# MLP steps ahead of value products, one load issue earlier, and V's second copy by DMA, in a fused block-sparse attention and MLP kernel

## The chip, the cores and the metric

The kernel runs on one core of a Trainium2 chip. The metric is the device time of one execution in microseconds (us). The kernel before takes 303.8 us (median of three runs, 303.51 to 305.62). A profile of one execution comes with each kernel. Its span is about 2 us shorter than the device time.

In the text PE is TensorE, ACT ScalarE, DVE VectorE, POOL GpSimd, and SPq the queue of SyncE, from which most DMAs are issued. L433 is line 433 of the kernel.

## The reference

Block-sparse attention for 4 batches x 8 heads x 768 rows x 64 columns, then a low-rank mixer over the sequence and an MLP, with residuals:

```python
scores = scale * q @ k.T                       # masked by block: window, first/last, sampled
attn   = softmax(where(mask, scores, -1e9))
x      = (attn @ v), heads side by side        # 4 x 768 x 512
h      = x.T @ U @ V                           # U 768x32, V 32x768
u      = x + h.T
out    = u + relu(u @ w_ch1) @ w_ch2           # 512 -> 2048 -> 512
```

## The kernel before

Heads go in pairs; a batch has four pairs, and there are 16. A pair has nine units. For each unit PE makes scores (`psc`), ACT their exps (`est`), DVE multiplies the exps by the mask (`est <- est, m`), and PE makes value products (`pav`). DVE normalises these (`rcp`, `xs`), POOL casts them (`xh`), PE makes the mixer's first product (`pa`), DVE casts that (`a`), PE makes the second (`ph`), and DVE adds (`xf`). The MLP of a finished batch (`pt`, relu to `tT`, `pch`, last add `of`) is cut into steps that fill PE during the next batch's attention. In the first batch no exps are multiplied by a mask: extra rows beside q and k (mask rows in `qa`, one-hot rows in `ka`) bring the mask into the score matmuls, and they too come by DMA.

Each engine works through its instructions in the order in which they were recorded, so the order of the Python statements is the schedule. From the second batch on, units go two to a group (the first eight singly), and this loop records a group:

```python
    while gi < len(groups) or work or beside:
        made = []
        for i, u in groups[gi] ...:                # PE: scores; ACT: exps
            scores(i, u, est); made.append((i, u, est))
        while beside and beside[0][0] <= gi:       # PE: ph;  DVE: two xf adds
            beside.popleft()[1]()
        for _ in range(...):                       # DVE: masks of the group before
            i, u, est = unmasked.popleft()
            mask_mul(u, est)
            if u == NU - 1:
                steps = pair_tail(i, *live.pop(i))
                for at, fn in zip((0, 1, 3), steps):   # values c=0, values c=1, pa
                    work.append((gi + at, fn))
                beside.append((gi + 4, steps[3]))      # ph
        unmasked.extend(made)
        ...                                        # loads, casts, transposes
        while work and work[0][0] <= gi:           # PE: pav or pa
            work.popleft()[1]()
        if gi in OPENS:
            fill.extend(mlp_steps(OPENS.index(gi)))
        if fill:                                   # PE: MLP steps
            run_fill(...)
```

The loads of the first pairs, and V, which is wanted at partitions 0 to 31 (`Vt`, `Vd`) and again at 64 to 95 (`Vd`):

```python
    def at_unit(i, u):
        if i == 0:
            if u == 0:
                cast(1, "q"); cast(1, "k"); cast(1, "v")     # POOL  (cut)
            if u == 1:
                ...
                issue(2, "qk")                               # SPq
                for h in range(2):                           # mask and one-hot rows, pair 1
                    keep(nc.sync.dma_start(out=qa[1][h][mrows[h], :], in_=qa[0][h][mrows[h], :]))
                    hot_rows(nc.sync, 1, h, D)
                issue(2, "v")
                for h in range(2):                           # V twice from memory
                    keep(nc.sync.dma_start(out=mvld[h * D : h * D + R], in_=moe_V))
                ...
        if u == 0 and i == 1:
            for o in (Vt[0:R], Vd[0:R]):
                keep(nc.gpsimd.tensor_copy(out=o, in_=mvld[0:R].rearrange("r (p t) -> r t p", t=T)))
        if u == 0 and i == 2:
            keep(nc.gpsimd.tensor_copy(out=Vd[D : D + R], in_=mvld[D : D + R].rearrange(...)))
```

The softmax here doesn't subtract the row's maximum and nothing guards it: scores larger than these inputs give would overflow.

Of the kernel before, what the change touches and what calls it, by code (L numbers as in the profile page):

```python
# [10 lines left out]
FP32 = mybir.dt.float32  # L11
# [10 lines left out]
def kernel(  # L22
# [12 lines left out]
    nc = tc.nc  # L35

    B, H, S, D = q.shape
    BLK = 32
    NB = S // BLK
    T = S // P  # L40
    HD = H * D
    HP = H // 2
    R = moe_U.shape[1]
# [51 lines left out]
    keep = tc.keep_in_program_order  # L95
# [50 lines left out]
    Vt = wpool.tile([P, T, P], FP16)  # L146
    Vd = wpool.tile([P, T, P], FP16)
    w1t = wpool.tile([P, NCC, CH], FP16)
    small = w1t[:, 0, 0 : S + 2 * NB]
    w2t = wpool.tile([P, NJJ, HD], FP16)  # L150
# [18 lines left out]
    def issue(i, names="qkv"):  # L169
        if i >= NPAIR:  # L170
            return
        for nm in names:
            keep(nc.sync.dma_start(out=new_ld(i, nm), in_=src_of(nm, i)))

    def cast(i, nm):
        if i >= NPAIR:
            return
        b, hp = divmod(i, HP)
        ld = lds.pop((i, nm))
        if nm == "v":  # L180
            keep(
                nc.gpsimd.tensor_copy(  # L182
                    out=vts[b % 2][:, 2 * hp : 2 * hp + 2, :, 0:D], in_=ld
                )
            )
            return
        st = stpool.tile([P, T, 2, D], FP16, tag="st" + nm, name=nm + "st")
        keep(nc.gpsimd.tensor_copy(out=st.rearrange("p t h d -> p h t d"), in_=ld))  # L188
        sts[i, nm] = st
# [34 lines left out]
    def hot_rows(eng, st, h, n):  # L224
# [5 lines left out]
            out=sbi[0:NB].rearrange("z r w -> z (r w)"),  # L230
            in_=sampled_blocks.bitcast(I32),
# [20 lines left out]
    def warm_pe(n):  # L252
        for _ in range(n):
            mm(
                warm.rearrange("p (r n) -> p r n", r=4), zeros,
                zeros[:, None, :].broadcast_to([P, 4, P]), True, True,
            )
# [5 lines left out]
            out=eq[0:NB],  # L263
# [7 lines left out]
            out=cb[0:NB],  # L271
            in_=eq[0:NB].rearrange("z r c -> z c r"),
# [6 lines left out]
            out=cbd[0:NB, :, 0:NB],  # L279
# [77 lines left out]
    cast(0, "v")  # L357

    uld = w2t[:, 3, 0 : 2 * T * R].bitcast(FP32)
    mvld = w2t[:, 0:3, :].rearrange("r j d -> r (j d)").bitcast(FP32)  # L360

    def load_w1(cc):
        keep(
# [331 lines left out]
    def at_unit(i, u):  # L695
        if (i, u) in MASKS:
            mask_tiles(MASKS.index((i, u)))
        if i == 0:
            if u == 0:
                warm_pe(2)  # L700
                cast(1, "q")
                cast(1, "k")
                cast(1, "v")
            if u == 1:
                turn_some(qst, pq, TQ, T)
                for h in range(2):
                    half_copy(nc.vector.tensor_copy, qa[0], h, pq, TQ, T)
                turn_some(kst, pk, TK, T)
                for h in range(2):
                    half_copy(nc.vector.tensor_copy, ka[0], h, pk, TK, T)  # L710
                give_back(pq, 0.0)
                give_back(pk, 0.0)
                give_back(warm, 0.0)
                issue(2, "qk")
                for h in range(2):
                    keep(
                        nc.sync.dma_start(
                            out=qa[1][h][mrows[h], :], in_=qa[0][h][mrows[h], :]
                        )
                    )  # L720
                    hot_rows(nc.sync, 1, h, D)
                issue(2, "v")
                for h in range(2):
                    keep(
                        nc.sync.dma_start(out=mvld[h * D : h * D + R], in_=moe_V)
                    )
                keep(
                    nc.sync.dma_start(
                        out=uld, in_=moe_U.rearrange("(p t) r -> p (t r)", t=T)
                    )  # L730
                )
            if u == 3:
                issue(3)
            if u == 6:
                cast(2, "q")
                cast(2, "k")
                cast(2, "v")
            if u == 4:
                turn_part(1, "q", 0)
                turn_part(1, "q", 1)  # L740
            if u in (5, 6):
                turn_part(1, "k", u - 5)
            return
        if u == 0:
            issue(i + 3)
            if i == 1:
                for h in range(2):
                    keep(
                        nc.gpsimd.tensor_copy(
                            out=Ut[:, :, h * D : h * D + R],  # L750
                            in_=uld.rearrange("p (t r) -> p t r", t=T),
                        )
                    )
                for o in (Vt[0:R], Vd[0:R]):
                    keep(
                        nc.gpsimd.tensor_copy(
                            out=o, in_=mvld[0:R].rearrange("r (p t) -> r t p", t=T)
                        )
                    )
            if i == 2:  # L760
                keep(
                    nc.gpsimd.tensor_copy(
                        out=Vd[D : D + R],
                        in_=mvld[D : D + R].rearrange("r (p t) -> r t p", t=T),
                    )
                )
        if (i, u) in WLOADS:
            WLOADS[i, u]()
        if u in (1, 2, 3, 4):
            turn_part(i + 1, "qk"[(u - 1) // 2], (u - 1) % 2)  # L770
        if u == 6:
            cast(i + 2, "q")
            cast(i + 2, "k")
        if u == 8:
            cast(i + 2, "v")
        for _ in range({0: 1, 5: 2, 6: 1, 7: 1}.get(u, 0)):
            if tails:
                tails.popleft()()
# [17 lines left out]
    def run_fill(us):  # L796
        state["debt"] += us
        while fill and state["debt"] > 0:
            cost, fn = fill.popleft()
            fn()  # L800
            state["debt"] -= cost
        if not fill:
            state["debt"] = min(state["debt"], 0.0)
# [34 lines left out]
    work = deque()  # L838
    beside = deque()
    gi = 0  # L840
    while gi < len(groups) or work or beside:
        made = []
        for i, u in groups[gi] if gi < len(groups) else []:
            b, hp = divmod(i, HP)
            if u == 0:
                if hp == 0:
                    start_batch(b)
                live[i] = ([], *new_x())
            est = new_est()
            live[i][0].append(est)  # L850
            scores(i, u, est)
            made.append((i, u, est))
        while beside and beside[0][0] <= gi:
            beside.popleft()[1]()
        for _ in range(len(unmasked) if gi >= SINGLE else 2 if gi >= OPENS[0] else 0):
# [4 lines that stand above are left out]
                for at, fn in zip((0, 1, 3), steps):  # L860
                    work.append((gi + at, fn))
                beside.append((gi + 4, steps[3]))
        unmasked.extend(made)
        for i, u, est in made:
            if u == 0:
                if i > HP:
                    turn_dma(i + 1, "q")
                    turn_dma(i + 1, "k")
                issue(i + 3)
            if u == 3:  # L870
                cast(i + 2, "q")
            if u == 5:
                cast(i + 2, "k")
            if u == 7:
                cast(i + 2, "v")
        if gi == 0:
            flush_value()
            tails.popleft()()
            flush_value()
        if gi == 1:  # L880
            flush_value()
            put_off.pop(0)()
        if gi == 2:
            tails.popleft()()
            tails.popleft()()
            put_off.pop(0)()
        if gi == 3:
            tails.popleft()()
            tails.popleft()()
        if gi == 5:  # L890
            tails.popleft()()
        if gi == 6:
            while put_off:
                put_off.pop(0)()
        while work and work[0][0] <= gi:
            work.popleft()[1]()
        if gi in OPENS:
            fill.extend(mlp_steps(OPENS.index(gi)))
        if fill:
            to_come = [n for n in OPENS if n > gi] or [gi + 1]  # L900
            run_fill(sum(c for c, _ in fill) / (to_come[0] - gi))
        if gi == 6:
            for nm in "qk":
                for part in range(2):
                    turn_part(HP + 1, nm, part)
        gi += 1
# [35 lines left out]
```

## Time and profile before

I divide the span at two points: where the first batch's MLP matmuls run on after their last wait (53.26 us), and where the last batch's begin (256.89 us).

| stage | from, to | length | what leads |
|---|---|---|---|
| first | 0 to 53.26 us | 53.3 us | loads, then exps on ACT |
| middle | to 256.89 us | 203.6 us | PE, with waits |
| last | to 302.2 us | 45.3 us | PE alone, MLP |

The page of the kernel before, part 1 (busy us, share of the span, instructions):

```profile
PE 282.2 (93%) x2749; PEld 158.2 (52%) x2749; DVE 178.2 (59%) x331; ACT 187.0 (62%) x248; POOL 94.2 (31%) x127
```

Windows of the kernel before, one line to a stage. After the stretch comes its length, then busy us (and instructions) of each engine, PE's granted clock, and DMA:

```profile
core 0: us, PE busy (x) PEld busy (x) DVE busy (x) ACT busy (x) POOL busy (x), PEclk, DMA share, GB/s
0.00:53.30 53.30, 47.08 (x565) 30.71 (x566) 36.44 (x83) 43.48 (x48) 33.08 (x52) 0.97 0.96 248
53.30:256.90 203.60, 193.57 (x1963) 105.79 (x1963) 136.96 (x241) 127.80 (x168) 61.12 (x76) 1.00 0.46 107
256.90:302.20 45.30, 41.51 (x224) 21.69 (x222) 4.82 (x7) 15.71 (x32) 0.00 (x0) 0.99 0.11 41
```

In the middle stage PE works 193.57 of 203.60 us: about 10 us can be had there without taking work from PE. The list of waits of PE says what they are (total, times, longest):

```profile
PE pav L129 <- DVE est L433: 9.3, 6, 1.6
PE psc L129 <- DMA ka<-onehot_const: 2.1, 2, 1.7
...
```

The timeline shows one of the six. Columns are start and length in us, engine, line, operation, shapes, and in brackets the idle time before. PE, kernel before:

```profile
168.44 0.60 PE L129 MATMUL psc<-qT,kT 64*128 64x512 f16 x4
168.88 0.33 PE L129 MATMUL ph<-a,Vd 64*128 64x128 f16 x6
169.14 0.33 PE L129 MATMUL pav<-vt,est 128*128 128x65 f16 x5
171.03 1.16 PE L129 MATMUL pav<-vt,est 128*128 128x65 f16 x31 [1.55 <-DVE est L433]
```

DVE in the same stretch:

```profile
166.81 0.69 DVE L609 TENSOR_TENSOR of<-xf,pch 128x512 f32<-128x512 f32 x1 [0.57 <-PE pch L129]
169.24 1.02 DVE L546 TENSOR_TENSOR xf<-xs,ph 128x384 f32<-128x384 f32 x2 [1.74 <-PE ph L129]
170.18 1.70 DVE L433 TENSOR_TENSOR est<-est,m 128x1024 f16<-128x1024 f16 x2
```

DVE stood idle for 1.74 us until ph came, did the two adds, and only then the mask multiplies, for which PE's sixth pav waits. This happens where a pair's ph falls into the group in which the next pair's first values are recorded, which is every second pair.

In the first stage ACT's exps have gaps. ACT, kernel before:

```profile
10.74 5.86 ACT L421 ACTIVATE est<-psc 128x1024 f16<-128x1024 f32 x6 [0.25 <-PE psc L129]
19.18 1.02 ACT L421 ACTIVATE est<-psc 128x1024 f16<-128x1024 f32 x1 [2.58 <-PE psc L129]
...
26.29 3.84 ACT L421 ACTIVATE est<-psc 128x1024 f16<-128x1024 f32 x4 [0.69 <-PE psc L129]
30.51 17.21 ACT L421 ACTIVATE est<-psc 128x1024 f16<-128x1024 f32 x18 [0.38 <-PE psc L129]
```

And the part of POOL's timeline that holds the first two casts of V, ahead of the casts of xh that pa needs:

```profile
21.40 1.56 POOL L756 CAST Vt<-w2t 32x768 f16<-32x768 f32 x1
22.91 1.57 POOL L756 CAST Vd<-w2t 32x768 f16<-32x768 f32 x1
24.43 0.95 POOL L473 CAST xh<-xs 128x384 f16<-128x384 f32 x2
```

Finally the third pair's q load (SPq) beside the second pair's q cast (POOL), from the timeline of all engines:

```profile
9.88 0.83 POOL L188 CAST qst<-qld 128x768 f16<-128x768 f32 x1
...
10.73 0.37 SPq L173 DMA_DIRECT2D qld<-in_q_dram  x1
```

The load issues 0.02 us after the cast ends: it waits for that cast's buffer.

### The profile page before, as it was taken

The numbers are of one execution on the slowest core, as the hardware profiler recorded it, in microseconds if no ns is written. First come the engines' busy times: TensorE is split into PE (matmuls) and PEld (weight loads), VectorE is DVE, ScalarE is ACT, GpSimd is POOL, SyncE is SP. The second block draws the span as 40 slices with busy tenths as digits, with TensorE's granted clock in tenths as the row PEclk, the third lists the DMA queues.
The fourth block names the chain that finished last, engine by engine and source line by source line (L and its number), as shares of the span: only waits on it lengthen the run. The fifth ranks groups of instructions, "written<-read, shape, count | busy, mean of one in ns | idle before, by whom it ended". The sixth has DMA issues, their size and how long they took to land.

```text
span 302.2 us, 6702 instructions
## 1 busy us (share of the span) xinstructions
PE 282.2 (93%) x2749; PEld 158.2 (52%) x2749; DVE 178.2 (59%) x331; ACT 187.0 (62%) x248; POOL 94.2 (31%) x127
## 2 busy tenths in 40 slices
PE   8979998899799899989999799989999799999994
PEld 2646775455555354546555444546565454665441
DVE  7736769777778585786585576686585623000111
ACT  4958999598686737586897355486897100676000
POOL 1549964023443444414244241413021201000000
PEclk9979999999999999999999999999999999999999
DMA  5898999860656666845346383415010423000111
GB/s 167 298 279 229 234 259 269 195 182 29 71 165 84 223 87 220 147 162 119 117 80 157 54 225 114 97 37 81 1 28 0 60 73 98 35 0 2 69 69 69
DMA packets 46221, 36.91 MB, mean 122 GB/s; under 512 B 27240, under 2 KB 42544, under 8 KB 46192
## 3 DMA queue, kind: packets, MB, share of 16 engines
q1 hardware_dynamic: 43016, 32.06, 40.7%
q0 software_dynamic: 2688, 4.19, 7.7%
q8 instruction: 21, 0.34, 0.5%
q10 hardware_dynamic: 488, 0.24, 0.3%
q14 instruction: 8, 0.07, 0.1%
HBM read 27.90 MB, written 6.29 MB: 113 GB/s over the span
## 4 chain that ended last, share of the span: by engine, by line
PE 82%; DVE 7%; ACT 4%; DMA 3%; issue 2%; SPq 1%; POOL 0%; ACTq 0%; DVEq 0%; POOLq 0%
PE pt L129 28%; PE pch L129 27%; PE psc L129 11%; PE pav L129 11%; ACT est L421 4%; DVE est L433 2%; PE pa L129 2%; DMA ka<-onehot_const 2%; DVE xf L546 1%; PE ph L129 1%; DMA id<-eye_const 1%; PE pturn L194 1%; DVE m L386 1%; PE warm L129 0%; PE pmk L129 0%
## 5 line engine op out<-in xcount | busy, mean ns | idle before, releaser
L421 ACT ACTIVATE est<-psc 128x1024 f16<-128x1024 f32 x144 | 139.3, 1023 | 40.6 <-PE psc L129 40.4
L129 PE MATMUL pt<-uT,w1t 128*128 128x384 f16 x512 | 88.7, 326 | 0.7 <-DVE uT L566 0.7
L129 PE MATMUL pch<-w2t,tT 128*128 128x512 f16 x384 | 87.5, 379 | 0.0
L433 DVE TENSOR_TENSOR est<-est,m 128x1024 f16<-128x1024 f16 x108 | 80.0, 782 | 2.4 <-ACT est L421 2.4
L589 ACT ACTIVATE tT<-pt 128x384 f16<-128x384 f32 x98 | 47.9, 492 | 47.1 <-PE pt L129 45.4
L129 PEld LDWEIGHTS <-w1t 128*128 128x128 f16 x512 | 48.1, 98 | 33.0 <-issue 3.1
L129 PE MATMUL pav<-vt,est 128*128 128x65 f16 x1152 | 48.6, 194 | 9.6 <-DVE est L433 9.3
L129 PEld LDWEIGHTS <-tT 128*128 128x128 f16 x384 | 35.7, 98 | 40.7 <-issue 0.7
L129 PEld LDWEIGHTS <-est 128*128 128x128 f16 x1152 | 43.1, 98 | 23.5 <-DVE est L433 10.8
L609 DVE TENSOR_TENSOR of<-xf,pch 128x512 f32<-128x512 f32 x24 | 16.5, 687 | 62.4 <-PE pch L129 62.4
L473 POOL CAST xh<-xs 128x384 f16<-128x384 f32 x30 | 21.0, 704 | 64.6 <-DVE xs L455 57.8
L551 POOL CAST uh<-xf 128x384 f16<-128x384 f32 x24 | 16.6, 718 | 73.7 <-issue 64.9
L129 PE MATMUL psc<-qT,kT 64*128 64x512 f16 (+1 forms) x288 | 33.5, 327 | 0.3 <-ACT est L421 0.3
L129 PE MATMUL psc<-qa,ka 128*128 128x512 f16 (+1 forms) x96 | 22.9, 335 | 2.5 <-DMA ka<-onehot_const 2.1
L129 PEld LDWEIGHTS <-kT 64*128 64x128 f16 x288 | 10.1, 94 | 21.7 <-issue 19.1
L592 DVE TENSOR_SCALAR tT<-pt 128x384 f16<-128x384 f32 x30 | 16.6, 556 | 7.3 <-PE pt L129 6.3
L455 DVE TENSOR_TENSOR xs<-pav,rcp 128x384 f32<-128x384 f32 x32 | 17.8, 557 | 1.9
L546 DVE TENSOR_TENSOR xf<-xs,ph 128x384 f32<-128x384 f32 x24 | 12.2, 550 | 11.1 <-PE ph L129 11.0
L450 DVE RECIPROCAL rcp<-pav 128x6 f32<-128x6 f32 x32 | 6.2, 194 | 18.7 <-PE pav L129 18.2
L188 POOL CAST kst<-kld 128x768 f16<-128x768 f32 x15 | 15.6, 1042 | 3.1 <-DMA kld<-in_k_dram 3.1
L182 POOL CAST vt<-vld 128x768 f16<-128x768 f32 x16 | 13.6, 851 | 6.1 <-DMA vld<-in_v_dram 6.1
L188 POOL CAST qst<-qld 128x768 f16<-128x768 f32 x15 | 14.7, 982 | 1.8 <-DMA qld<-in_q_dram 1.3
(58 smaller groups left out, 114.2 us busy)
## 6 DMA issues: line engine op xcount, KB each, us to landing
vld<-in_v_dram SPq DMA_DIRECT2D x16, 384.0 KB, 5.5
out_dram<-of SPq DMA_DIRECT2D x24, 256.0 KB, 2.0
qld<-in_q_dram SPq DMA_DIRECT2D x15, 384.0 KB, 4.3
kld<-in_k_dram SPq DMA_DIRECT2D x15, 384.0 KB, 4.7
w1t<-in_moe_w_ch_dram POOLq DMA_DIRECT2D x4, 512.0 KB, 8.6
w2t<-in_moe_w_ch_dram POOLq DMA_DIRECT2D x4, 512.0 KB, 17.2
qld<-in_q_dram SPq DMA_DIRECT2D x1, 256.0 KB, 2.9
kld<-in_k_dram SPq DMA_DIRECT2D x1, 256.0 KB, 4.3
```

Source lines behind the costliest of these rows:

```text
L129: nc.tensor.matmul(out, lhsT, rhs, start=start, stop=stop, skip_group_check=loose)
L182: nc.gpsimd.tensor_copy(out=vts[b % 2][:, 2 * hp : 2 * hp + 2, :, 0:D], in_=ld)
L188: keep(nc.gpsimd.tensor_copy(out=st.rearrange("p t h d -> p h t d"), in_=ld))
L421: keep(nc.scalar.activation(out=est, in_=psc, func=AF.Exp, scale=0.125))
L433: keep(nc.vector.tensor_tensor(out=o, in0=o, in1=m, op=ALU.mult))
L455: nc.vector.tensor_tensor(out=o.rearrange("p j (h d) -> p j h d", h=2), in0=pav[:, :, :, 0:D], in1=rcp[:, :, :, None].broadcast_to([P, 3, ...
L473: keep(nc.gpsimd.tensor_copy(out=xh[:, 3 * c : 3 * c + 3, :], in_=x3))
L546: nc.vector.tensor_tensor(out=u3, in0=xs[:, tc3, :], in1=phs[c], op=ALU.add)
L551: keep(nc.gpsimd.tensor_copy(out=uh[:, tc3, :], in_=u3))
L589: keep(nc.scalar.activation(out=dst, in_=pt, func=AF.Relu))
L592: keep(nc.vector.tensor_scalar_max(out=dst, in0=pt, scalar1=0.0))
L609: keep(nc.vector.tensor_add(out=of, in0=xfs[b][:, sc, :], in1=pchs[sc]))
```

## The change

The intent is, first, to give PE ready work between ph and the values; second, to let the third pair's loads go earlier; third, to take two casts and a load away, by copying V to its second place by DMA. The diff, with cuts:

```diff
@@ at_unit, i == 0
                 warm_pe(2)
+                issue(2, "qk")
                 cast(1, "q")
...
-                issue(2, "qk")
                 for h in range(2):          # mask and one-hot rows
...
-                for h in range(2):
-                    keep(nc.sync.dma_start(out=mvld[h * D : h * D + R], in_=moe_V))
+                keep(nc.sync.dma_start(out=mvld, in_=moe_V))
@@ at_unit, u == 0
-                for o in (Vt[0:R], Vd[0:R]):
-                    keep(nc.gpsimd.tensor_copy(out=o, in_=mvld[0:R]...))
-            if i == 2:
-                keep(nc.gpsimd.tensor_copy(out=Vd[D : D + R], in_=mvld[D : D + R]...))
+                keep(nc.gpsimd.tensor_copy(out=Vt[0:R, :, :], in_=mvld...))
+        if i == 2 and u == 0:
+            for h in range(2):
+                keep(nc.sync.dma_start(out=Vd[h * D : h * D + R], in_=Vt[0:R]))
@@ the group loop
-        while work and work[0][0] <= gi:
-            work.popleft()[1]()
         if gi in OPENS:
             fill.extend(mlp_steps(OPENS.index(gi)))
         if fill:
             ...
+        while work and work[0][0] <= gi:
+            work.popleft()[1]()
```

More of the change, by code (lines that the diff above doesn't have):

```diff
@@ L359 @@
     uld = w2t[:, 3, 0 : 2 * T * R].bitcast(FP32)
-    mvld = w2t[:, 0:3, :].rearrange("r j d -> r (j d)").bitcast(FP32)
+    mvld = w2t[0:R, 0:3, :].rearrange("r j d -> r (j d)").bitcast(FP32)
     def load_w1(cc):
@@ L722, in at_unit @@
                 issue(2, "v")
-                for h in range(2):
-                    keep(
-                        nc.sync.dma_start(out=mvld[h * D : h * D + R], in_=moe_V)
-                    )
+                keep(nc.sync.dma_start(out=mvld, in_=moe_V))
                 keep(
@@ L753, in at_unit @@
                     )
-                for o in (Vt[0:R], Vd[0:R]):
-                    keep(
-                        nc.gpsimd.tensor_copy(
-                            out=o, in_=mvld[0:R].rearrange("r (p t) -> r t p", t=T)
-                        )
-                    )
-            if i == 2:
                 keep(
                     nc.gpsimd.tensor_copy(
-                        out=Vd[D : D + R],
-                        in_=mvld[D : D + R].rearrange("r (p t) -> r t p", t=T),
-                    )
-                )
+                        out=Vt[0:R, :, :],
+                        in_=mvld.rearrange("r (p t) -> r t p", t=T),
+                    )
+                )
+        if i == 2 and u == 0:
+            for h in range(2):
+                keep(nc.sync.dma_start(out=Vd[h * D : h * D + R], in_=Vt[0:R]))
         if (i, u) in WLOADS:
```

## The prediction

> **What bounds the kernel now.** The page: TensorE (PE) busy 282.2 of 302.2 us (93%), ScalarE 62%, VectorE 59%, GpSimd 31%; the chain of waits lies 82% on PE. Three stages: to 53 us attention alone, led by exps back to back on ScalarE (30.5 to 44 us); to 250 us PE interleaves scores, values, mixer products and MLP steps; then the last batch's MLP, PE alone. In the middle stage the list of waits shows one real PE loss: value products (pav) waiting for the mask multiply (est), 9.3 us in 6 waits, mostly 1.55. The timeline shows them alike (near 77, 105, 134, 170, 203, 237 us): scores, ph, five pav, then idle, while VectorE does two xf adds (0.55 us each), which need ph, and then the mask multiply (0.73 us). The Trainium skill (Perfetto Trace Analysis, "Optimization Strategy") says that consistent bubbles can mean too few buffers; here the trace names an ordering instead.
>
> **What the change does.**
> 1. MLP steps before values and pa. After ph now stand 1.3 to 2.6 us of ready MLP work (pch 8 x 0.217 us, or 2 to 4 pt steps of 0.65 us), while the first mask is ready 1.75 us after ph. Five of the six waits should vanish; one, with 1.3 us between, shrinks to 0.4 us: 8.9 us gained, all on the chain.
>    Given back: pa now stands last in its group, so its VectorE cast (0.29 us, often behind a relu or add of 0.56 to 0.69) has only the next 0.54 us of scores to hide behind before ph: about 0.1 us in each of 10 pairs, about 0.5 and 0.7 us in the stream's last two, where no scores stand between. PSUM banks: evacuations finish in time by my reading. Together 2.3 us with margin.
> 2. Third pair's loads. The DMA queue's emitted order and waits are unchanged: the q load takes the second pair's buffer and still waits for its cast (ends 10.71 us; load issues at 10.73). Worth 0.
> 3. V by DMA. Removes one V load (about 0.9 us of issue) and two GpSimd casts of 1.57 us (22.9 and 30.4 us); adds two small copies, wanted only after 70 us. xh and uh casts come up to 1.5 us earlier; PE waited for them only 0.3 and 0.2 us, and ScalarE had gaps of 0.69 and 0.38 us before its unbroken run at 30.5 us. Worth 0.5 us; then exps bound the stage.
>
> **Sum.** 303.8 - 8.9 + 2.3 - 0.5 = 296.7 us, range 294.0 to 300.2. Chances: faster by over 2% (below 297.7) 0.63, within 2% 0.36, slower 0.01.
>
> **What would show it.** Right: pav waiting for est falls from 9.3 to under 1.5 us; PE stays near 282 us busy, its share rises to 95%; ph waiting for the a cast appears with 1 to 2 us; the last MLP keeps its 42 us; GpSimd busy falls 3 us; ScalarE's unbroken run starts 0.5 us earlier; the third q load still issues right after the second pair's q cast. Wrong: pav waits for masks elsewhere (normalisations now stand ahead of them), pt or pch wait for a bank, psc waits for exps, or the first stage moves over 1 us.
>
> **What would make it wrong.** New VectorE queueing: it is over 80% busy at 80 to 100 and 120 to 140 us (windows) and gets more relus; ph waits of 0.4 us in every pair would leave 299 to 300 us.

## The result, and the profile after

The changed kernel takes 294.8 us (median of 4 runs, 294.40 to 295.13) against 304.61 us of the kernel before in the same rounds. The ratio is 0.9678, with a 95% interval of 0.9634 to 0.9722.

| stage | before | changed | difference |
|---|---|---|---|
| first | 53.26 | 50.99 | -2.27 us |
| middle | 203.63 | 196.93 | -6.70 us |
| last | 45.3 | 45.3 | 0.0 us |

The page of the changed kernel, part 1:

```profile
PE 282.2 (96%) x2749; PEld 162.1 (55%) x2749; DVE 189.8 (65%) x347; ACT 178.2 (61%) x232; POOL 96.4 (33%) x125
```

Its windows:

```profile
0.00:51.00 51.00, 47.58 (x565) 30.93 (x566) 36.12 (x83) 43.25 (x48) 29.41 (x50) 1.00 0.99 257
51.00:248.00 197.00, 193.16 (x1963) 109.55 (x1963) 148.94 (x258) 119.32 (x152) 66.95 (x76) 1.00 0.45 111
248.00:293.20 45.20, 41.44 (x224) 21.65 (x222) 4.76 (x7) 15.68 (x32) 0.00 (x0) 0.99 0.11 41
```

PE does the same 193 us of work in the middle stage in 197 us. Sixteen relus went from ACT to DVE. PE's waits in the changed kernel:

```profile
PE ph L129 <- DVE a L505: 3.0, 4, 1.7
...
PE pav L129 <- DVE est L433: 0.2, 1, 0.2
...
```

The old wait is gone and a new one of 3.0 us is there. PE's timeline shows both: first a group in which ph and values meet, as at 168 us before, then the longest of the new waits:

```profile
161.59 0.61 PE L129 MATMUL psc<-qT,kT 64*128 64x512 f16 x4
162.04 0.34 PE L129 MATMUL ph<-a,Vd 64*128 64x128 f16 x6
162.32 1.90 PE L129 MATMUL pch<-w2t,tT 128*128 128x512 f16 x8
164.05 1.30 PE L129 MATMUL pav<-vt,est 128*128 128x65 f16 x36
...
175.17 0.50 PE L129 MATMUL pa<-xh,Ut 128*128 128x128 f16 x6
175.60 0.61 PE L129 MATMUL psc<-qT,kT 64*128 64x256 f16 x6
177.91 0.34 PE L129 MATMUL ph<-a,Vd 64*128 64x128 f16 x6 [1.70 <-DVE a L505]
```

DVE in these two stretches:

```profile
162.40 1.02 DVE L546 TENSOR_TENSOR xf<-xs,ph 128x384 f32<-128x384 f32 x2 [0.41 <-PE ph L129]
163.34 1.70 DVE L433 TENSOR_TENSOR est<-est,m 128x1024 f16<-128x1024 f16 x2
...
176.97 0.69 DVE L609 TENSOR_TENSOR of<-xf,pch 128x512 f32<-128x512 f32 x1 [2.45 <-DMA out_dram<-of]
177.58 0.28 DVE L505 CAST a<-pa 128x128 f16<-128x128 f32 x1
```

In the first stretch DVE's order is what it was, but eight pch matmuls stand over it. In the second, the cast of a stands behind an add that waits 2.45 us for one of two output buffers. The timeline of SPq tells why: that buffer's store was issued after a transpose of uT that waited for its uh, two more transposes, and three loads.

```profile
164.52 2.33 SPq L556 DMA_TRANSPOSE uT<-uh  x1
166.94 1.24 SPq L207 DMA_TRANSPOSE qT<-qst  x1
168.23 1.29 SPq L207 DMA_TRANSPOSE kT<-kst  x1
...
171.26 6.76 SPq L612 DMA_DIRECT2D out_dram<-of  x3
```

In the first stage, ACT of the changed kernel has lost the gaps of 2.58 and 0.69 us:

```profile
9.11 2.10 ACT L421 ACTIVATE est<-psc 128x1024 f16<-128x1024 f32 x2 [1.80 <-PE psc L129]
...
12.76 15.19 ACT L421 ACTIVATE est<-psc 128x1024 f16<-128x1024 f32 x16 [0.25 <-PE psc L129]
28.29 17.17 ACT L421 ACTIVATE est<-psc 128x1024 f16<-128x1024 f32 x18 [0.34 <-PE psc L129]
```

Its first exp comes at 9.11 us, not at 7.30 as before, though nothing up to there differs. The two traces started differently, so the first stage needs more than one pair of traces. Below, a trace with its first exp at 7.0 to 7.3 us has the early start, one with it at 9.11 us the late start.

### The profile page after: what moved, and what is told of

It reads as the page before. It is cut to its first block, busy times and chain, and to the rows that moved or that the text cites. A ratio compares the mean times of both kernels' runs of the same rounds, so it can differ in the third digit from the quotient of the medians.

```text
span 293.2 us, 6701 instructions
## 1 busy us (share of the span) xinstructions
PE 282.2 (96%) x2749; PEld 162.1 (55%) x2749; DVE 189.8 (65%) x347; ACT 178.2 (61%) x232; POOL 96.4 (33%) x125
## 4 chain that ended last, share of the span: by engine, by line
PE 76%; DVE 8%; ACT 5%; POOL 3%; issue 2%; SPq 2%; DMA 2%; POOLq 0%; DVEq 0%; ACTq 0%
PE pt L129 26%; PE pch L129 25%; PE psc L129 10%; PE pav L129 9%; ACT est L421 5%; DVE est L433 3%; PE warm L129 2%; DMA out_dram<-of 2%; PE ph L129 1%; DVE tT L592 1%; SPq L207 1%; PE pa L129 1%; SPq L556 1%; PE pturn L194 1%; DVE of L609 1%
## 5 line engine op out<-in xcount | busy, mean ns | idle before, releaser
L433 DVE TENSOR_TENSOR est<-est,m 128x1024 f16<-128x1024 f16 x108 | 85.4, 836 | 0.0
L589 ACT ACTIVATE tT<-pt 128x384 f16<-128x384 f32 x82 | 39.3, 495 | 34.1 <-PE pt L129 32.8
L129 PEld LDWEIGHTS <-est 128*128 128x128 f16 x1152 | 44.1, 97 | 11.1 <-issue 0.5
L473 POOL CAST xh<-xs 128x384 f16<-128x384 f32 x30 | 23.1, 772 | 76.9 <-DVE xs L455 74.5
L129 PE MATMUL pav<-vt,est 128*128 128x65 f16 x1152 | 46.5, 193 | 0.3 <-DVE est L433 0.2
L592 DVE TENSOR_SCALAR tT<-pt 128x384 f16<-128x384 f32 x46 | 23.8, 545 | 1.2 <-PE pt L129 0.6
L129 PE MATMUL psc<-qa,ka 128*128 128x512 f16 (+1 forms) x96 | 22.1, 331 | 0.3 <-DVE qa L341 0.2
L188 POOL CAST kst<-kld 128x768 f16<-128x768 f32 x15 | 16.5, 1100 | 2.9 <-DMA kld<-in_k_dram 2.9
L188 POOL CAST qst<-qld 128x768 f16<-128x768 f32 x15 | 16.5, 1101 | 1.9 <-DMA qld<-in_q_dram 1.8
```

The lines of the kernel that those rows point to most:

```text
L129: nc.tensor.matmul(out, lhsT, rhs, start=start, stop=stop, skip_group_check=loose)
L188: keep(nc.gpsimd.tensor_copy(out=st.rearrange("p t h d -> p h t d"), in_=ld))
L433: keep(nc.vector.tensor_tensor(out=o, in0=o, in1=m, op=ALU.mult))
L473: keep(nc.gpsimd.tensor_copy(out=xh[:, 3 * c : 3 * c + 3, :], in_=x3))
L589: keep(nc.scalar.activation(out=dst, in_=pt, func=AF.Relu))
L592: keep(nc.vector.tensor_scalar_max(out=dst, in0=pt, scalar1=0.0))
```

## The experiments

Twelve runs were made, all correct; one repeats the kernel before, one the changed kernel. Times are medians; "before" is the kernel before in the same rounds. Of the timed executions one of six of e7 was slow (295.81 us) and is left out of its ratio; the two repeats are single executions, whose state is unknown. "First pt matmul" means here the first MLP matmul after its last wait, which ends the first stage. One more build, the changed kernel with three output buffers instead of two, is said not to have fitted the on-chip memory; it did not run.

### The order alone (e1_mlp_first)

```diff
-        while work and work[0][0] <= gi:
-            work.popleft()[1]()
         if gi in OPENS: ...
         if fill: ...
+        while work and work[0][0] <= gi:
+            work.popleft()[1]()
```

> The kernel before with the first part of the change alone: MLP steps ahead of values and mixer products, loads and V as before. The changed kernel's trace is 2.3 us shorter than before's up to the first MLP matmul, 6.7 us shorter from there to the last batch's MLP. Theory A (order alone makes the middle stage; V makes the first): from the first to the last batch's first pt matmul 196 to 198 us, pav waiting for est under 0.5 us, ph waiting for the a cast about 3.0 us; first stage as before; time 6 to 7.5 us under before, ratio 0.976 to 0.980. Theory B (the first stage's 2.3 us are chance of one trace, and the order makes nearly all): ratio 0.968 to 0.972. If the V part mattered to the middle stage, the middle would stay above 199 us.

Measured: 296.45 us against 303.67, ratio 0.9757 (0.9729 to 0.9784). Middle stage 196.56 us; ph waits 2.6 us for a, and pav for est 0.2 us. The middle stage is the order's doing, as theory A had it, and the V part is not needed for it.

### V by DMA alone (e2_v_dma)

```diff
-                for h in range(2):
-                    keep(nc.sync.dma_start(out=mvld[h * D : h * D + R], in_=moe_V))
+                keep(nc.sync.dma_start(out=mvld, in_=moe_V))
...              # one cast of three, two copies by DMA, as in the change
```

> The kernel before with the V part alone (one V load, one GpSimd cast, two copies by DMA). By the prediction 0.3 to 0.7 us faster, ratio 0.9977 to 0.999, from earlier xh and uh casts. Theory A: the V part makes all 2.3 us of the first stage, ratio 0.991 to 0.994, and its trace shows the first pt matmul near 51 us, without ScalarE's gap of 2.6 us before the exp at 19 us. Theory B: chance, the first pt matmul anywhere between 51 and 53.3 us and ratio above 0.996. Middle stage unchanged: pav waiting for est near 9.3 us.

Measured: 303.11 us against 303.67, ratio 0.9967 (0.9936 to 0.9997). Middle stage 203.62 us with pav's 9.3 us as before. The first pt matmul came at 52.20 us, and ACT's gap of 2.58 us near 19 us stayed. So neither theory fits whole: the V part does not take that gap away, but it is worth about 1 us. The interval (0.1 to 1.9 us) still holds the prediction's 0.5; the section on all traces has more on this.

### The load issue alone (e3_issue)

```diff
                 warm_pe(2)
+                issue(2, "qk")
                 cast(1, "q")
...
-                issue(2, "qk")
```

> The kernel before with the load issue alone moved. The built program has the same instructions, waits and wait values on every engine, so this is a control of noise: ratio 1.000 within 0.4%, and a second trace of the same program. If its first pt matmul comes near 53.3 us again, and the second pair's one-hot rows land near 18.5 us again, the kernel before has that wait as a rule; if it comes near 51 us, the wait was chance of one trace.

Measured: 304.10 us against 303.67, ratio 1.0015 (0.9986 to 1.0044). The trace has the stages of before again (53.42 and 203.62 us). This part is worth nothing: in the two traces every engine has the same instructions in the same order, so moving the statement changed nothing that is executed.

### pa ahead of the MLP steps, values behind (e4_pa_ahead)

Against the changed kernel:

```diff
-                for at, fn in zip((0, 1, 3), steps):
+                for at, fn in zip((0, 1), steps):
                     work.append((gi + at, fn))
+                ahead.append((gi + 3, steps[2]))
...
+        while ahead and ahead[0][0] <= gi:
+            ahead.popleft()[1]()
         if gi in OPENS: ...
         if fill: ...
         while work and work[0][0] <= gi: ...
```

> The changed kernel, but the mixer product pa stands ahead of the MLP steps again while the values stay behind them. Theory: the 3.0 us of ph waiting for the a cast in the changed kernel come from pa standing last. Then that wait falls under 0.5 us, pav waiting for est stays under 0.5 us, and the time is 2 to 3 us under the changed kernel: ratio to before 0.958 to 0.962. Rival: VectorE is full there and the wait moves elsewhere (pav for est, or pt for a bank): ratio 0.966 to 0.970.

Measured: 292.33 us against 303.67, ratio 0.9619 (0.9591 to 0.9648). The wait of ph for a is gone from the list, and the middle stage is 193.26 us, 3.67 us under the changed kernel's. The rival fails: nothing took the wait's place. An add still waits 1.42 us for an output buffer, but the cast of a now stands ahead of it.

### Rows of the second pair ahead of the third pair's loads (e5_hot_first)

```diff
                 warm_pe(2)
+                for h in range(2):
+                    keep(nc.sync.dma_start(out=qa[1][h][mrows[h], :], in_=qa[0][h][mrows[h], :]))
+                    hot_rows(nc.sync, 1, h, D)
                 issue(2, "qk")          # the loop is taken out of u == 1
```

> The kernel with pa ahead of the MLP steps (292.33 us), and the second pair's mask rows and one-hot rows issued ahead of the third pair's loads. The queue stood idle from 6.8 us to the third q load at 10.4 to 10.7 us because that load waits for a cast; the rows wait for nothing later than 7.4 us, so they should issue by 10 us and land before 15 us instead of 16.9 to 18.5 us. Theory (the rows' landing holds back the second pair's scores, and TensorE's idle time there then halves its clock for 3.4 us): no wait of psc for these rows, no halved clock near 18 us in any start, time 0.5 to 2.5 us lower, ratio to before 0.954 to 0.960. Rival (the DMA engines are the limit there and only the order changes): the q and k loads land later, the third pair's casts and transposes wait, ratio stays 0.961 to 0.963.

Measured: 292.04 us against 303.76, ratio 0.9601 (0.9566 to 0.9635), which is the kernel without this edit (e4, 0.9619) within its interval. Each trace gives the landing of one one-hot row only: here that of the first, issued at 8.18 us, which took 7.2 us and landed near 15.4 us; in e4 that of the second, issued at 12.72 us, which took 6.3 us and landed near 19.0 us. The two are not the same row, so it is likely but not shown that both came earlier; the one known did not land before 15 us, and PE's 0.5 us of waits for the rows in e4 are gone. The third pair's q and k casts came 0.7 and 0.9 us later than in e4 (17.15 and 18.66 us), as the rival expected. As e4's trace had the late start, in which these waits are short, there was little to gain, and the time does not tell theory from rival. The Trainium skill (DMA: Bandwidth & Descriptors, "Queues, rings and completion order") says that on each DMA engine a queue's descriptors are consumed in ring order. The landings of this trace follow the order of issue: the second pair's k and v loads, issued ahead of the rows at 5.79 and 6.30 us, released their casts at 13.05 and 14.54 us, before the row landed.

### Masks ahead of the xf adds on DVE, in the kernel before (e6_masks_first)

```diff
-        while beside and beside[0][0] <= gi:
-            beside.popleft()[1]()
         for _ in range(...):
             ... mask_mul(u, est) ...
+        while beside and beside[0][0] <= gi:
+            beside.popleft()[1]()
         unmasked.extend(made)
```

> The kernel before, with one swap: ph and its xf adds are recorded behind the mask multiplies of the group instead of ahead. TensorE's order is the same as before instruction for instruction; only VectorE's order differs. Theory (the 9.3 us are an ordering on VectorE: masks whose inputs are ready stand behind adds that wait for ph): pav waiting for est falls under 1 us with no MLP step moved, middle stage 194 to 196 us against 203.6, ratio 0.968 to 0.974, and no wait of ph for a. Rival (the masks are late because VectorE or ScalarE has too much to do there, and MLP steps help by filling time): the wait stays above 5 us, ratio above 0.985.

Measured: 292.97 us against 303.76, ratio 0.9643 (0.9609 to 0.9677). Middle stage 192.71 us, 10.92 us under before, and no wait of PE for est is listed any more; the middle stage and the ratio are better than was expected. This is the plainest test of the cause: PE's order is the same, instruction for instruction, and no MLP step moved. PE, this kernel, in a group of the kind shown above:

```profile
163.19 0.33 PE L129 MATMUL ph<-a,Vd 64*128 64x128 f16 x6
163.45 1.31 PE L129 MATMUL pav<-vt,est 128*128 128x65 f16 x36
164.60 1.89 PE L129 MATMUL pch<-w2t,tT 128*128 128x512 f16 x8
```

And DVE, which does the masks while it waits for ph:

```profile
161.73 1.28 DVE L433 TENSOR_TENSOR est<-est,m 128x1024 f16<-128x1024 f16 x2
163.56 1.02 DVE L546 TENSOR_TENSOR xf<-xs,ph 128x384 f32<-128x384 f32 x2 [0.54 <-PE ph L129]
```

The rival (too much work on DVE or ACT) falls. The swap is also worth more than the order change, since it brings no new wait: the middle stage is 4.2 us shorter than the changed kernel's.

### Masks first, V by DMA and rows first together (e7_masks_v_hot)

The edits of e6, e2 and e5 on the kernel before.

> The kernel before with three small moves: masks ahead of the xf adds on VectorE, V by DMA, and the second pair's mask and one-hot rows issued ahead of the third pair's loads; MLP steps and pa stay where they were. If the VectorE swap is as good as moving the MLP steps, the middle stage is 194 to 196 us (193.3 with pa ahead and values behind) and the time within 1.5 us of the kernel with pa ahead and rows first: ratio 0.955 to 0.965. If later xf adds hold PSUM banks and make pt or pch wait, ratio above 0.968.

Measured: 291.51 us against 303.76, ratio 0.9578 (0.9551 to 0.9604). The middle stage is 192.72 us, so later xf adds hold no bank for long. The lowest median.

### V by DMA, with the second load of V kept (e8_second_load)

```diff
                 keep(nc.sync.dma_start(out=mvld, in_=moe_V))
+                keep(nc.sync.dma_start(out=w2t[D : D + R, 0:3, :]..., in_=moe_V))   # read by nothing
```

> The V part alone, but with the second load of V kept in its place in the queue (into the old spot, where nothing reads it). The V part alone gave ratio 0.9967 and, in its trace, ScalarE's exps without gap from 21.6 to 32 us, where the control had gaps of 0.59 and 0.37 us. Theory (the two casts fewer on GpSimd give the gain): the gaps stay away and the first pt matmul comes within 0.4 us of 52.2 us in a start with the first exp near 7.3 us; ratio 0.995 to 0.998. Rival (the load fewer gives it, by 0.9 to 1.3 us of issue): the gaps return, first pt near 53.3 us, ratio 0.998 to 1.002.

Measured: 302.44 us against 303.76, ratio 0.9941 (0.9916 to 0.9966). The trace had the late start (first exp at 9.11 us), not the one that the expectation speaks of; its first pt matmul came at 51.99 us. Two gaps of 0.33 and 0.38 us were left on ACT after 24 us, where the kernel before in a late start has 1.60 and 0.37 (e9). So most of the V part's gain comes with the load still there, from the two casts fewer; this rests on one trace. In time this kernel was even a little faster than the V part alone (0.9941 against 0.9967, intervals overlapping), so nothing shows that the load is worth anything. The table below takes this up.

### Both kernels once more, for the start (e9_before_again, e10_after_again)

No edit.

> The kernel before, unchanged, once more, for its first stage. So far ten traces show two starts: TensorE's full clock from about 4 us (first exp near 7.3 us, then the second pair's scores wait for the one-hot rows and the clock is halved near 18 us) or from about 10 us (first exp at 9.1 us, no such wait). Expected: one of the two, first pt matmul 52.6 to 53.5 us in either, middle stage 203.6 us. If the start is a property of the kernel, the early one again.

> The changed kernel, unchanged, once more. If the start is chance, either can come; first pt matmul 51 to 52.3 us in either, so 1.0 to 2.0 us ahead of the kernel before in the same start; middle stage 196.9 us, ph waiting for a near 3.0 us.

Measured, one run each: 304.33 and 296.22 us. The kernel before now had the late start (first exp 9.11 us, first pt 53.35 us), the changed kernel the early one (7.05 and 52.33 us, with the wait for the one-hot rows, 2.3 us). So the start is chance and not the kernel's. The middle stages were 203.62 and 196.45 us. PE's list of waits of the kernel before in its late start has a line that its early start had with 0.3 us only:

```profile
PE pa L129 <- POOL xh L473: 1.2, 1, 1.2
```

### Masks first and V by DMA, without the rows (e11_masks_v)

> Masks ahead of the xf adds and V by DMA, without the rows issued early: it tells whether those rows are worth anything (0.9578 with them). Theory after the last runs (the rows land when the backlog of loads ahead of them is through, wherever they stand in the queue): no difference, ratio 0.955 to 0.961, middle stage 192.7 us. Rival: the rows issued early save the halved clock of the early start, ratio 0.961 to 0.966 without them.

Measured: 292.10 us against 303.84, ratio 0.9596 (0.9554 to 0.9638); middle stage 192.71 us. It lies within the interval of e7 (0.9551 to 0.9604), so the rows' place is not shown to be worth anything. Its profile had the early start and the halved clock; neither trace with the rows first had that start, so what they would do there stays open. Nor is the theory about the landing shown: the landings known with the rows issued first (near 15.4 us in e5, 14.6 us in e7) speak rather against it.

### The last add in place (e12_in_place)

Against the changed kernel:

```diff
-                of = opool.tile([P, HD], FP32, tag="of", name="of")
+                of = xfs[b][:, sc, :]
```

> The changed kernel with the last add of the MLP written in place (into xf) and stored from there, so that it needs none of the two output buffers; the order on every engine is the changed kernel's. In the changed kernel's traces one add waits 2.0 to 2.5 us for an output buffer whose store stood behind transposes and loads in the DMA queue, the a cast stands behind that add, and ph waits 1.2 to 1.7 us for the cast. Theory: the output buffer is the cause; the wait of ph for a falls from 2.5 to 3.0 us to 1.2 to 1.4 us, the add waits for no store, the middle stage goes from 196.5 to 196.9 us down to 194.9 to 195.6 us, ratio to before 0.961 to 0.967. Rival: the cast is late for another reason (VectorE full), and the wait stays above 2.2 us.

Measured: 293.96 us against 304.36, ratio 0.9658 (0.9623 to 0.9693). No add waits for a store; ph waits 1.3 us for a; middle stage 195.33 us. DVE, this kernel, at the place of the changed kernel's longest wait:

```profile
175.50 0.69 DVE L609 TENSOR_TENSOR xf<-xf,pch 128x512 f32<-128x512 f32 x1 [0.85 <-PE pch L129]
176.11 0.28 DVE L505 CAST a<-pa 128x128 f16<-128x128 f32 x1
```

In whole runs the gain on the changed kernel (0.9678) is within the intervals, so the traces decide: the output buffer was the cause of the longest wait, and cost 1.1 to 1.6 us of the middle stage (196.45 and 196.93 against 195.33).

### The stages of all traces

Middle stage, us. The kernel before, its repeat and the control, which are the same program, agree to 0.01 us, so differences of a tenth can be read; the changed kernel and its repeat, where an add waits for a store, differ by 0.48 us:

| kernel | middle |
|---|---|
| before, before again, control, V alone, V alone with second load | 203.62 to 203.63 |
| changed, changed again | 196.93, 196.45 |
| order alone | 196.56 |
| changed, in place | 195.33 |
| pa ahead; the same with rows first | 193.26, 193.27 |
| masks first; with V; with V and rows | 192.71, 192.71, 192.72 |

First stage (time of the first pt matmul after its last wait), us, by start. In order, the traces are: V as before, early: before, e3; late: e1, e6, e9; second load kept: e8; by DMA, early: e2, e10, e11; late: changed, e4, e12; rows first: e5, e7.

| V part | early start | late start |
|---|---|---|
| as before | 53.26, 53.42 | 52.66, 53.27, 53.35 |
| by DMA, second load kept | | 51.99 |
| by DMA | 52.20, 52.33, 52.08 | 50.99, 51.65, 51.11 |
| by DMA, rows first | | 51.30, 51.19 |

Within one kind of start, the V part's means differ by 1.14 us (53.34 less 52.20) in the early and 1.84 us (53.09 less 51.25) in the late one. With the second load kept it is 1.1 us in the late start. The remaining 0.7 us are the load's or chance: one trace does not tell, and the late traces with V as before differ by 0.7 us among themselves.

## Why the prediction was right

**The time.** 296.7 us was predicted with a range of 294.0 to 300.2; 294.8 us was measured. The mechanism and the range held; the point was 1.9 us high. Against the kernel before in the same rounds the gain was 9.8 us (9.0 us between the two traces), where 7.1 us was predicted.

**The middle stage: the net is right, its two terms are not.** -8.9 and +2.3 make -6.6 us; the trace gives -6.70. But with the wait removed and nothing given back, the stage falls by 10.4 us (pa ahead) to 10.9 us (masks first), not by 8.9. The reason is in how idle time is counted. A pav lasts 194 ns on average, while 31 of them take 1.16 us, so they start about 32 ns apart. Idle is counted from the modelled end of the last matmul, not from when the next could have started. One wait listed as 1.55 us so costs about 0.16 us more, and six cost 1.0 us more than the 9.3 us listed. That is an estimate from these durations; about 0.6 us of the 10.9 stay unexplained. The Trainium skill (Perfetto Trace Analysis, "Tensor Engine Instruction (MATMUL, LD_WEIGHTS)") says that the end of a matmul in a profile is estimated, not observed, which agrees.

The term given back was 2.3 us in the prediction. Taking pa out of its last place regains 3.67 us. The list says 3.0 us in 4 waits. Of these, 1.0 us in two waits lie at the end of the stream, where 1.2 was predicted; one of 0.2 us is in a group full of relus; the other eight pairs have none, where 0.1 us each was predicted. The longest, 1.7 us, was not foreseen at all: a full output buffer, held by a store that stood behind transposes in the DMA queue, and felt on PE because DVE works in order. The test in place shows it. The two errors have opposite signs and nearly cancel: that the net came out right to 0.1 us is luck.

**Third pair's loads: worth 0**, as predicted. The control has the same waits and ratio 1.0015. In the changed kernel the load issues at 10.41 us, just after the second pair's q cast again.

**V by DMA: the mechanism is right, the size is too small.** The term that was mis-sized is the 0.5 us (0.3 to 0.7 in the expectation of e2). It came from one trace with the early start, where PE waited only 0.27 us for xh, since a wait for the one-hot rows and a halved clock had already put it behind. In the late start the same wait is 1.0 to 1.5 us (order alone 1.0, before again 1.2, masks first 1.5). The part's traces give 1.1 and 1.8 us. Timed alone, it gives ratio 0.9967, and 0.9941 with the second load kept. Timed on top of the order change (e1 against the changed kernel, the load issue being worth nothing) it takes the ratio from 0.9757 to 0.9678, some 2.4 us, and there the intervals do not overlap. Against the predicted 0.5 us the traces' 1.1 to 1.8 us are 0.6 to 1.3 us more, which makes up much of the 1.9 us. The rest of the pair's 2.27 us in the first stage goes with the difference in start; how much of it is chance of one trace is not shown.

**What the prediction said would be seen.** The wait of pav for est fell to 0.2 us; the wait of ph for a appeared, with 3.0 us where 1 to 2 was named; PE stayed at 282.2 us busy; its share is 96%; the last stage kept its length. The sign "ScalarE's unbroken run starts 0.5 us earlier" was off: it started at 12.76 us with one gap, or, counted from the gap before 18 exps, 2.2 us earlier (28.29 against 30.51); the first stage moved by more than the 1 us that I had named as a sign of error. The sign "GpSimd busy falls 3 us" failed as it stood: it rose from 94.2 to 96.4 us. With V alone it fell to 90.8; the order alone raised it to 99.8, because casts of the same shape took longer (that of q 982 ns before, 1100 with the order alone); why they did is not shown. The feared move of pav's wait to other places did not come, nor did waits for banks.

## What to carry to other kernels

When an engine waits for a second one, first look at whether the second had the needed work ready and was itself blocked on something else: swapping two statements on VectorE gained more than giving TensorE other work to do, and brought no new wait. When something is moved to the end of a group, follow what stands in front of its consumers on every in-order engine, and in the DMA queue, with the number of buffers between. And before costing a move of a statement in a program whose engines each keep their own order, check whether any engine's order or wait changes at all.

## What the Trainium skill lacked or had wrong

- TensorE: Matmul & The Clock Gate, "Part 1: The HAM clock gate": it gives the rise to full clock at about 4 us of sustained matmuls, within 500 ns from run to run. Here the clock records of fourteen traces begin, at full clock, at 3.9 to 4.6 us of the span in five and at 9.4 to 10.5 us in nine, for the same opening instructions. The first matmul came at 0.99 us, and in the changed kernel PE was busy for all 8.39 us from there to the start of its record. The chain of waits shows it too: the same four warm-up matmuls took 0.86 us in the kernel before and 1.71 us in the changed one.
- The same page, "HAM oscillation": its rule is to have no PE idle gap over about 3.4 us. Here one idle gap of 1.67 us, from 15.9 to 17.6 us of the kernel before, was followed by 3.41 us at half clock (windows: granted clock 0.50 from 18 to 20 us), and every trace with the early start has the same after a gap of 1.56 to 2.01 us. The gap's length alone does not decide it: the changed kernel's wait of 1.70 us before 177.91 us left the clock at 1.00, as did the six waits of 1.55 us in the kernel before. What made the difference is not shown. The length of the halved stretch, 3413 ns in all five clock records, agrees with the window that the page gives in Part 1.
- Perfetto Trace Analysis, "Optimization Strategy": for consistent bubbles the one cause that it names, as a possible one, is too few buffers. Here six like bubbles, 9.3 us as listed, went away by swapping two statements on VectorE, with every buffer as it was (203.6 to 192.7 us).
- The same page has the estimated end of a matmul but not what follows for reading idle time: six waits listed as 9.3 us were worth 10.4 to 10.9 us.
